# Retention followed by a Fourier mixing block on one core: the eight sums of the second weight's blocks are placed among the third batch's last products

## The chip, the cores and the metric

The kernel runs on one core of a Trainium2 chip. TensorE (PE in the profile) multiplies matrices into PSUM, VectorE (DVE), ScalarE (ACT) and GpSimd (POOL) work element by element, SyncE (SP) issues most transfers. Each engine takes its own instructions strictly in the order of the program, and engines wait for one another by semaphores. The metric is the device time of one execution in microseconds; the median over several runs counts.

## The reference

Four batches of 768 tokens with 8 heads of 64 go through a decaying recurrence, then a Fourier mixing with a normalization, then a two-layer MLP with a residual. Cut to what matters:

```
state = gamma * state + k_t v_t^T ;  y_t = scale * q_t . state      # per head
u  = x + real(fft2(x))                                               # x: y of all heads, 768 x 512
un = (u - mean(u)) / sqrt(var(u) + 1e-6)
out = u + max(un @ w_ch1, 0) @ w_ch2                                 # w_ch1 512 x 2048, w_ch2 2048 x 512
```

## The kernel before

**Batches in a pipeline.** While TensorE runs the MLP of batch b, the recurrence and the mixing of batch b+1 are made between its products. The MLP of batches 0 to 2 is plain: `h_unit` (L1083) makes one block of 128 hidden rows for 384 tokens (four products into one PSUM tile, then a ReLU to `ht16`), and `ch_unit` (L1120) multiplies the hidden rows with the second weight `w216` for 128 tokens: 16 products of 512 columns into the PSUM tile `psc`, and then one VectorE addition at L1131 (`ob` = `psc` times the reciprocal deviation plus `u`) and a store. Three such tiles close a half batch, so batch 2 ends with 48 products and three additions at L1131.

**The last batch is different.** Nothing is left to overlap with it, and its second product is made in a form with seven block products instead of eight (Strassen's scheme in Winograd's form), in three groups g of 256 tokens each. For each group:

- `hp_unit` (L1165), n = 0 to 7: eight products into the PSUM tile `psh` (two hidden blocks, n and n + 8, times 256 tokens), then a ReLU on ScalarE at L1180 into `hg`. For n = 7 the ReLU is cut in two: ScalarE takes the first half (128x256), VectorE the second at L1183. After n = 2, 5 and 7, VectorE forms four differences and sums of the token blocks at L1193 (`s1`, `s2`, `s4`, and one written back into `hg`).
- `p_unit` (L1196), k = 1, 4, 5, 6, 2, 7, 3: seven block products of eight matrix products each (L1217). k = 1, 2 and 3 take a block of `w216` as it is; k = 4, 5, 6 and 7 take one of the sums below. k = 2 goes on in the PSUM tile of k = 1, k = 7 in that of k = 6, and k = 3 in that of k = 5, so each of them must wait until VectorE has read the earlier result (L1222).

**The sums of the weight's blocks.** `wsum_unit` (L1152) makes four differences of 256-column blocks of `w216` (k = 1, 2, 3, 4), each in two parts of four rows of blocks: eight VectorE instructions at L1161, 128x1024 elements of 16 bits each. They are chained: 2 needs 1, 4 needs 2; 3 stands alone. The result tiles come from `inp`, the pool of 11 buffers in which q, k and v arrive; the products k = 4 to 7 of all three groups read them. They depend on nothing of the batch but a free buffer.

**Two halves of the mixing.** The rows of `u` of batch b that the first group needs (blocks kb = 0, 1, 2) are made during batch b - 1. Blocks 3, 4 and 5 are made at the start of batch b's own MLP: `s2_unit` (L991) has four small products into `pq` (L1010), two ScalarE copies (L1012, L1013), two VectorE instructions (L1017, L1020), and two GpSimd additions of x (L1038, L1040); `norm_unit` (L1044) then has the VectorE statistics (L1050, L1051) and the normalization on ScalarE (L1052, `un`); `unT_unit` transposes it by a DMA. For the last batch these blocks 3, 4, 5 stand between the products of its first group, beside the ReLUs and the sums.

**What sets the order.** The units are written out by hand, with a due time each: a stream is a list of units with a start and an end in units of a batch, and `emit` sorts all of them by due time. Then the framework's scheduler arranges the instructions of each engine by its own estimate; it may pull an instruction far forward when nothing holds it. `held` (L148) prevents that for a unit: each of its instructions gets an order dependency on the instruction that stands before it on its engine at the time it is written. (In the program before, `held` is used for the casts of q, k and v.)

**PSUM.** `ps_pm` has three buffers, used in turn by `psc` and `psh`: the three `psc` tiles that close batch 2 are followed, in the same three buffers, by the first three `psh` tiles of batch 3. `ps_g` has five buffers for everything else.

Of the kernel before, what the change touches and what calls it, by code (L numbers as in the profile page):

```python
# [53 lines left out]
LD0, LD1 = (0.223, 0.312), (-0.370, 0.140)  # L54
HT0 = (0.666, 0.693, 0.632, 0.590)
NPE = 2
WS = (0.0, 0.12)
KD = (2, 3)
NT = 0.6
ACT_ROWS = ((2, 5, 6, 7, 8, 9, 10, 14), (0, 3, 6, 7, 9, 10, 11, 12, 14, 15))  # L60
# [3 lines left out]
def kernel(  # L64
# [83 lines left out]
    def held(unit):  # L148
        def run():
            ins = tc.nc.cur_bb.bb.instructions  # L150
            n0 = len(ins)
            unit()
            for n in range(n0, len(ins)):
                m = n - 1
                while m >= 0 and ins[m].engine != ins[n].engine:
                    m -= 1
                if m >= 0:
                    tc.add_manual_dep(ins[n], ins[m].name,
                                      mybir.DependencyInfo(mybir.DependencyClass.NoSync,
                                                           mybir.DependencyReason.DATA),  # L160
                                      reason="casts in turn")
        return run
# [893 lines left out]
    def rstd_unit(b, rt):  # L1056
        def run():
            stats = lb[b]["st"]
            if b == 0 and rt == 0:
                bn_unit(0)()  # L1060
            sl = slice(3 * rt, 3 * rt + 3)
            nc.scalar.activation(stats[:, sl, 2:3], stats[:, sl, 1:2], AF.Sqrt, bias=epsT,
                                 scale=1.0)
            nc.vector.reciprocal(out=stats[:, sl, 3:4], in_=stats[:, sl, 2:3])
        return run

    def unT_unit(b, kb):
        def run():
            un, unT = lb[b].pop(("un", kb)), lb[b]["unT"]
            if b > 1 or b and kb >= 3:  # L1070
                nc.sync.dma_start_transpose(unT[:, :, kb * P:(kb + 1) * P], un)
                return
            pst = ps_g.tile([P, 4, P], f16, tag="g", name="pst", padded_shape=[P, 8, P])
            for cb in range(4):
                nc.tensor.transpose(pst[:, cb, :], un[:, cb * P:(cb + 1) * P], ident16)
            if (kb % 2 == 0) != (b == 0 and kb < 3):
                nc.vector.tensor_copy(unT[:, :, kb * P:(kb + 1) * P], pst)
            else:
                nc.scalar.copy(unT[:, :, kb * P:(kb + 1) * P], pst)
        return run  # L1080
# [61 lines left out]
    def spare(n, name):  # L1142
        return flat(inp.tile([P, 2, NCH, D], f32, tag="in32", name=name))[:, 0:n]
# [5 lines left out]
    def half_of(w, fh, eh, n0, n1):  # L1149
        return w[:, 8 * fh + n0:8 * fh + n1, 256 * eh:256 * eh + 256]  # L1150

    def wsum_unit(k, part):  # L1152


        def run():
            n0, n1 = 4 * part, 4 * part + 4
            t = seven["t", k, part] = spare(4 * 256, "wsum").rearrange("p (n m) -> p n m", n=4)
            a, b = {1: ((0, 1), (0, 0)), 2: ((1, 1), None), 3: ((1, 1), (0, 1)),
                    4: ((1, 0), None)}[k]
            in1 = half_of(w216, *b, n0, n1) if b else seven["t", k // 2, part]  # L1160
            nc.vector.tensor_tensor(out=t, in0=half_of(w216, *a, n0, n1), in1=in1,  # L1161
                                    op=ALU.subtract)
        return run

    def hp_unit(b, g, n):  # L1165

        def run():
            unT = lb[b]["unT"]
            if (g, n) == (0, 0):
                seven["s4"] = spare(8 * P, "s4").rearrange("p (n k) -> p n k", n=8)  # L1170
            psh = ps_pm.tile([P, 2, 256], f32, tag="pm", name="psh")
            for t in range(2):
                fb = n + 8 * t
                for cb in range(4):
                    nc.tensor.matmul(psh[:, t], w116[:, cb, fb * P:(fb + 1) * P],  # L1175
                                     unT[:, cb, g * 256:(g + 1) * 256],
                                     start=(cb == 0), stop=(cb == 3))
            for t0, t1, eng in (((0, 1, "a"), (1, 2, "v")) if n == 7 else ((0, 2, "a"),)):
                if eng == "a":
                    nc.scalar.activation(hg[:, n, t0:t1], psh[:, t0:t1], AF.Relu, bias=0.0,  # L1180
                                         scale=-1.0)
                else:
                    nc.vector.tensor_scalar(out=hg[:, n, t0:t1], in0=psh[:, t0:t1], scalar1=-1.0,  # L1183
                                            scalar2=0.0, op0=ALU.mult, op1=ALU.max)
            if n in (2, 5, 7):
                sl = slice({2: 0, 5: 3, 7: 6}[n], n + 1)
                a11, a12 = hg[:, sl, 0, 0:P], hg[:, sl, 1, 0:P]
                a21, a22 = hg[:, sl, 0, P:256], hg[:, sl, 1, P:256]
                s1, s2, s4 = sg[:, 0, sl], sg[:, 1, sl], seven["s4"][:, sl]
                for out_, x, y, op in ((s1, a21, a22, ALU.add), (s2, s1, a11, ALU.subtract),  # L1190
                                       (s4, a12, s2, ALU.subtract),
                                       (a21, a11, a21, ALU.subtract)):
                    nc.vector.tensor_tensor(out=out_, in0=x, in1=y, op=op)  # L1193
        return run
# [167 lines left out]
    def mix_units(b, kbs, s0, s1, u0, u1):  # L1362
        def turn(j):
            def run():
                s2_unit(b, kbs[j])()
                if j:
                    norm_unit(b, kbs[j - 1])()
            return run
        t = s1 + NT * min((s1 - s0) / 3, u1 - s1)
        return [([turn(j) for j in range(3)], s0, s1), ([norm_unit(b, kbs[2])], t, t),  # L1370
                ([unT_unit(b, kb) for kb in kbs], u0, u1)]
# [21 lines left out]
    streams = []  # L1393
    for b in range(B):
        majors = []
        if b == B - 1:
            for g in range(3):
                majors += [hp_unit(b, g, n) for n in range(8)]
                if g < 2:
                    majors.append(rstd_unit(b, g))  # L1400
                majors += [p_unit(b, g, k) for k in (1, 4, 5, 6, 2, 7, 3)]
            streams.append(([wsum_unit(k, part) for part in range(2) for k in (1, 2, 3, 4)],
                            b + WS[0], b + WS[1]))
        elif b == 0:
            for kb in range(3):
                if kb:
                    majors.append(unT_unit(0, kb))
                majors += [h0_unit(kb, g) for g in range(4)]
        else:
            majors += [h_unit(b, 0, fb) for fb in range(NFB)]  # L1410
        if b < B - 1:
            majors.append(rstd_unit(b, 0))
            majors += [ch_unit(b, 0, rb3, part) for rb3 in range(3) for part in range(4)]
            majors += [h_unit(b, 1, fb) for fb in range(NFB)]
            majors.append(rstd_unit(b, 1))
            majors += [ch_unit(b, 1, rb3, part) for rb3 in range(3) for part in range(4)]
        streams.append((majors, b, b + 1.0))
        streams += mix_units(b, [3, 4, 5], *(b + t for t in (DM0 if b == 0 else DM1)))
        if b + 1 < B:
            steps = attn_steps(b + 1)  # L1420
            if b == 0:
                streams.append(([load_unit(1, i, 6) for i in range(4)], LD0[0], LD0[1]))
                streams.append(([qt_zeros], 0.1, 0.15))
                streams.append(([half_tables], HT0[0], HT0[1]))
                streams.append(([pad_unit], HT0[2], HT0[3]))
                ts = TS0
            else:
                streams.append(([load_unit(b + 1, i) for i in range(4)], b + LD1[0], b + LD1[1]))
                n = [len(u) for u in steps[1:]]
                ts = list(TS1[:2]) + [TS1[2] + TS1[3] * sum(n[:j]) / sum(n) for j in range(6)]  # L1430
            streams.append((steps[0], b + ts[0], b + ts[1]))
            streams += [(u, b + ts[j + 2], b + ts[j + 3]) for j, u in enumerate(steps[1:])]
            end = b + ts[-1]
            da = DA0 if b == 0 else DA1
            sums = [s1_unit(b + 1, e, cb) for cb in range(2) for e in range(2)]
            sums.insert(1, g0_unit(b + 1, (1, 2)))
            streams.append((sums, end + da[0], end + da[1]))
            streams += mix_units(b + 1, [0, 1, 2], *(end + t for t in da[2:]))
# [31 lines left out]
```

## Time and profile before

| what | us |
|---|---|
| median of 3 runs | 242.04 (241.83 to 242.31) |
| the profiled execution | 243.38 |
| its span (first to last instruction) | 240.6 |
| TensorE busy in the span | 226.1 |
| VectorE busy | 189.6 |
| ScalarE busy | 125.2 |
| GpSimd busy | 82.0 |

The profile of one execution is read by several views. The page gives the busy time of each engine, and the chain of work that ended last, followed back from the last instruction. The view of waits says which engine stood idle until which other had finished. The timeline lists each engine's instructions in order of time, merged where equal ones follow each other: the start, the time from the first start to the last end, the engine, line and operation, the tiles, the count, and in brackets the idle time before it and what ended it. The windows give the busy time of each engine in a chosen stretch. In these timelines one instruction's time overlaps the next one's by some 0.05 to 0.1 us, so the step from start to start is a little shorter than the time of a single instruction.

The last batch begins in this span at 194.63 us, when the 48 products that close batch 2 are done; its first group ends at 212.78 us.

### The profile page before, as it was taken

How to read it: one execution, taken by the hardware profiler on the slowest of the kernel's cores; microseconds unless marked ns; L12 is line 12 of the kernel's file. 1: busy time of each engine (PE TensorE's matmuls, PEld its weight loads, DVE VectorE, ACT ScalarE, POOL GpSimd, SP SyncE). 2: the span in 40 equal slices, each digit the busy share in tenths (PEclk: the TensorE clock that was granted, in tenths of full speed). 3: DMA queues.
4: the chain of work that ended last, by engine and by line, in shares of the span. 5: the costliest groups of instructions: out<-in, count | busy, mean ns of one | idle time of the engine just before them, and what ended most of it. 6: DMA issues, size and time to landing. Idle time of an engine off the chain costs nothing.

```text
span 240.6 us, 5573 instructions
## 1 busy us (share of the span) xinstructions
PE 226.1 (94%) x2127; PEld 154.8 (64%) x2127; DVE 189.6 (79%) x472; ACT 125.2 (52%) x272; POOL 82.0 (34%) x148
## 2 busy tenths in 40 slices
PE   0888999999999999999899999999999998899994
PEld 0366779756774656665567446655675477688883
DVE  8699987948898889977886759997886529968473
ACT  5989759675864544931147405822356336251430
POOL 7378802575300197850001817930003204200000
PEclk9999999999999999999999999999999999999999
DMA  7999999999999489979999587675100240140202
GB/s 169 236 269 260 207 207 207 217 245 247 243 232 213 78 193 217 186 142 123 256 277 210 112 177 203 131 120 159 44 3 0 70 131 0 40 115 1 90 0 87
DMA packets 101241, 36.78 MB, mean 153 GB/s; under 512 B 91488, under 2 KB 98528, under 8 KB 101216
## 3 DMA queue, kind: packets, MB, share of 16 engines
q1 hardware_dynamic: 96992, 32.25, 63.5%
q0 software_dynamic: 4224, 4.19, 10.6%
q8 instruction: 16, 0.26, 0.5%
q14 instruction: 9, 0.07, 0.1%
HBM read 27.26 MB, written 6.29 MB: 139 GB/s over the span
## 4 chain that ended last, share of the span: by engine, by line
PE 79%; DVE 7%; DMA 6%; POOL 2%; ACT 2%; issue 1%; SPq 1%; POOLq 0%; DVEq 0%
PE psc L1127 23%; PE psh L1088 21%; PE ps L1217 7%; PE psh L1175 6%; PE psh L1105 3%; PE wkA L665 3%; DMA qTz<-q16z 3%; DMA v<-in_v_dram 3%; PE ps L848 3%; PE wkY L719 2%; PE pq L1010 1%; PE ps L828 1%; PE wkY L715 1%; PE wkK L684 1%; SPq L217 1%
## 5 line engine op out<-in xcount | busy, mean ns | idle before, releaser
L1127 PE MATMUL psc<-w,ht 128*128 128x512 f16 x288 | 67.7, 379 | 0.0
L1088 PE MATMUL psh<-unT,w 128*128 128x384 f16 x320 | 59.5, 326 | 0.0
L1038 POOL TENSOR_TENSOR u<-u,x 128x256 f32<-128x256 f32 x21 | 13.8, 655 | 109.7 <-DVE u L1017 97.4
L1127 PEld LDWEIGHTS <-ht 128*128 128x128 f16 x288 | 27.2, 98 | 26.5
L1088 PEld LDWEIGHTS <-w 128*128 128x128 f16 x320 | 29.9, 98 | 15.9 <-DMA unT<-un 0.4
L1092 ACT ACTIVATE ht<-psh 128x384 f16<-128x384 f32 x46 | 22.3, 489 | 24.1 <-PE psh L1088 23.6
L668 DVE TENSOR_TENSOR atm<-wkA,maskp 128x512 f16<-128x512 f32 x36 | 23.6, 682 | 2.1 <-PE wkA L665 2.1
L1180 ACT ACTIVATE ht<-psh 128x512 f16<-128x512 f32 (+1 forms) x24 | 13.6, 569 | 19.3 <-PE psh L1175 17.1
L1052 ACT ACTIVATE un<-u,stats 128x512 f16<-128x512 f32 x21 | 14.7, 718 | 15.5 <-DVE stats L1051 9.0
L1175 PE MATMUL psh<-unT,w 128*128 128x256 f16 x192 | 22.6, 273 | 0.0
L1131 DVE SCALAR_TENSOR_TENSOR ob<-psc,stats,u 128x512 f32<-128x512 f32 x18 | 13.4, 744 | 9.9 <-PE psc L1127 9.7
L1094 DVE TENSOR_SCALAR ht<-psh 128x384 f16<-128x384 f32 x34 | 18.7, 550 | 2.7 <-PE psh L1088 2.5
L1175 PEld LDWEIGHTS <-w 128*128 128x128 f16 x192 | 18.6, 98 | 2.5 <-DMA unT<-un 0.2
L694 DVE SCALAR_TENSOR_TENSOR s<-s,gk,wkK 128x128 f16<-128x128 f16 x48 | 16.2, 337 | 2.3 <-ACT s L690 1.6
L727 ACT ACTIVATE x<-wkY,gexp 128x384 f16<-128x384 f32 x24 | 12.9, 580 | 9.0 <-PE wkY L719 8.9
L1050 DVE BATCH_NORM_STATS2 bst<-u 128x6 f32<-128x512 f32 x21 | 14.4, 687 | 3.2 <-POOL u L1040 2.8
L1217 PEld LDWEIGHTS <-ht 128*128 128x128 f16 x144 | 13.8, 98 | 4.1 <-ACT ht L1180 1.5
L439 POOL TENSOR_SCALAR kd<-k,gexp 128x384 f16<-128x384 f32 x24 | 13.8, 585 | 3.7 <-DMA k<-in_k_dram 3.6
L1193 DVE TENSOR_TENSOR ht<-ht 128x384 f16<-128x384 f16 (+1 forms) x27 | 9.2, 369 | 6.1 <-ACT ht L1180 5.9
L665 PE MATMUL wkA<-qTz,kT 128*128 128x256 f16 x72 | 13.2, 272 | 0.6 <-DMA qTz<-q16z 0.6
L1040 POOL TENSOR_TENSOR u<-u,x 128x256 f32<-128x256 f32 x21 | 13.4, 640 | 1.0 <-DVE u L1020 1.0
L1217 PE MATMUL ps<-wsum,ht 128*128 128x256 f16 x96 | 12.1, 273 | 0.4 <-DVE ht L1183 0.4
(190 smaller groups left out, 396.3 us busy)
## 6 DMA issues: line engine op xcount, KB each, us to landing
q<-in_q_dram SPq DMA_DIRECT2D x16, 384.0 KB, 5.9
k<-in_k_dram SPq DMA_DIRECT2D x16, 384.0 KB, 5.6
v<-in_v_dram SPq DMA_DIRECT2D x16, 384.0 KB, 5.9
out_dram<-ob SPq DMA_DIRECT2D x21, 256.0 KB, 2.7
w<-in_moe_w_ch_dram POOLq DMA_DIRECT2D x8, 512.0 KB, 10.7
out_dram<-ob SPq DMA_DIRECT2D x5, 128.0 KB, 2.0
unT<-un SPq DMA_TRANSPOSE x15, 2.5
kT<-kd SPq DMA_TRANSPOSE x10, 3.0
```

The lines of the kernel that those rows point to most:

```text
L439: kc = nc.gpsimd.tensor_scalar(out=kd[:, :, h2, :], in0=k32[:, h2], scalar1=gkd[:, h0 + h2:h0 + h2 + 1], scalar2=1.0, op0=ALU.mult, op1=AL ...
L665: mm = nc.tensor.matmul(wk[:, c2], st["kT"][:, c, :], st["qT"][:, :, c, :], start=True, stop=True)
L668: nc.vector.tensor_tensor(out=st["atm"][:, 2 * part:2 * part + 2], in0=wk, in1=maskp[:, PAIR_ORDER[i]].unsqueeze(1).to_broadcast([P, 2, 2, ...
L694: nc.vector.scalar_tensor_tensor(out=s16[:, c], in0=s16[:, c - 1], scalar=gk2[:, hp:hp + 1], in1=wk[:, c - c0], op0=ALU.mult, op1=ALU.add)
L1050: nc.vector.bn_stats(bst, u[:, kb, :])
L1052: nc.scalar.activation(un, u[:, kb, :], AF.Identity, bias=stats[:, kb, 0:1], scale=-1.0)
L1088: nc.tensor.matmul(psh, w116[:, cb, fb * P:(fb + 1) * P], unT[:, cb, rt * 384:(rt + 1) * 384], start=(cb == 0), stop=(cb == 3))
L1092: nc.scalar.activation(ht16[:, fb, :], psh, AF.Relu, bias=0.0, scale=-1.0)
L1094: nc.vector.tensor_scalar(out=ht16[:, fb, :], in0=psh, scalar1=-1.0, scalar2=0.0, op0=ALU.mult, op1=ALU.max)
L1127: nc.tensor.matmul(psc, ht16[:, fb, rb3 * P:(rb3 + 1) * P], w216[:, fb, :], start=(fb == 0), stop=(fb == NFB - 1))
L1175: nc.tensor.matmul(psh[:, t], w116[:, cb, fb * P:(fb + 1) * P], unT[:, cb, g * 256:(g + 1) * 256], start=(cb == 0), stop=(cb == 3))
L1217: nc.tensor.matmul(ps[:, c0:c1], lhsT, rhs[:, c0:c1], start=bool(new and n == 0), stop=(n == 7), skip_group_check=True)
```

## The change

The due times of the eight sums go from 0.0 to 0.12 after the start of the last batch to 0.12 to 0.02 before it, and each sum is held behind the instruction that stands before it on VectorE.

```diff
@@ -54,7 +54,7 @@
 HT0 = (0.666, 0.693, 0.632, 0.590)
 NPE = 2
-WS = (0.0, 0.12)
+WS = (-0.12, -0.02)
 KD = (2, 3)
@@ -1399,7 +1399,7 @@
-            streams.append(([wsum_unit(k, part) for part in range(2) for k in (1, 2, 3, 4)],
+            streams.append(([held(wsum_unit(k, part)) for part in range(2) for k in (1, 2, 3, 4)],
                             b + WS[0], b + WS[1]))
```

## The prediction

> **What bounds the kernel now.** First the page: which engine is full.
>
> ```profile
> PE 226.1 (94%) x2127; PEld 154.8 (64%) x2127; DVE 189.6 (79%) x472; ACT 125.2 (52%) x272; POOL 82.0 (34%) x148
> ```
>
> TensorE sets the end, so moving VectorE work pays only where TensorE waits for it. The view of waits, cut to TensorE from 60 us on, shows where that is; these three are all of 0.3 us or more.
>
> ```profile
> PE ps L1217 <- ACT ht L1180: 1.2, 1, 1.2
> PE wkA L665 <- DMA qTz<-q16z: 0.6, 1, 0.6
> PE ps L1217 <- DVE ht L1183: 0.4, 1, 0.4
> ```
>
> The windows give the stretches around the first and the third.
>
> ```profile
> 184.27:194.63 10.36, 10.36 (x52) 4.70 (x50) 5.50 (x13) 3.04 (x7) 2.62 (x5) 1.00 0.32 87
> 202.31:212.78 10.47, 8.81 (x78) 7.02 (x76) 9.61 (x27) 3.51 (x7) 1.91 (x3) 1.00 0.21 39
> 212.78:237.02 24.24, 24.20 (x230) 21.57 (x227) 15.99 (x43) 8.02 (x15) 0.00 (x0) 1.00 0.14 50
> ```
>
> The columns behind the stretch are its length, then the busy time of PE, PEld, DVE, ACT and POOL. While the third batch's last products run, TensorE is full and VectorE is busy 5.50 of 10.36 us; in the first group of the last batch TensorE loses 1.66 us and VectorE is busy 9.61 of 10.47; behind that TensorE is full again. So the change acts on the 10.47 us. TensorE's timeline of that stretch:
>
> ```profile
> 196.61 1.91 PE L1175 MATMUL psh<-unT,w 128*128 128x256 f16 x16
> ...
> 202.31 0.93 PE L1217 MATMUL ps<-w,ht 128*128 128x256 f16 x7
> 203.07 0.38 PE L1217 MATMUL ps<-wsum,ht 128*128 128x256 f16 x2
> 204.68 0.28 PE L1217 MATMUL ps<-w,ht 128*128 128x256 f16 x1 [1.22 <-ACT ht L1180]
> ...
> 212.78 4.97 PE L1175 MATMUL psh<-unT,w 128*128 128x256 f16 x44
> 217.59 1.04 PE L1217 MATMUL ps<-w,ht 128*128 128x256 f16 x8
> ```
>
> From the last two rows one product of 256 columns takes (217.59 - 212.78)/44 = 0.109 us from start to start. Up to 212.78 there are 56 block products and 20 for the next group, 76 x 0.109 = 8.3 us of work: 2.2 us is idle, which is all that this change could save. The long wait is for the ScalarE half of the ReLU n = 7. Why that is late stands in three engines' timelines, VectorE's first:
>
> ```profile
> 200.12 0.68 DVE L1161 TENSOR_TENSOR wsum<-w 128x1024 f16<-128x1024 f16 x1
> 200.72 0.47 DVE L1017 SCALAR_TENSOR_TENSOR u<-pq,g,qn 128x256 f32<-128x256 f32 x1
> 201.12 0.68 DVE L1161 TENSOR_TENSOR wsum<-w,wsum 128x1024 f16<-128x1024 f16 x1
> 201.72 0.47 DVE L1020 SCALAR_TENSOR_TENSOR u<-pq,g,qn 128x256 f32<-128x256 f32 x1
> 202.11 0.68 DVE L1050 BATCH_NORM_STATS2 bst<-u 128x6 f32<-128x512 f32 x1
> 202.71 0.74 DVE L1161 TENSOR_TENSOR wsum<-w 128x1024 f16<-128x1024 f16 x1
> 203.38 0.17 DVE L1051 BATCH_NORM_AGGREGATE stats<-bst 128x2 f32<-128x6 f32 x1
> 203.47 0.65 DVE L1161 TENSOR_TENSOR wsum<-w,wsum 128x1024 f16<-128x1024 f16 x1
> 204.04 0.35 DVE L1193 TENSOR_TENSOR ht<-ht 128x384 f16<-128x384 f16 x1
> ```
>
> ScalarE's and, below it, GpSimd's:
>
> ```profile
> 203.63 0.72 ACT L1052 ACTIVATE un<-u,stats 128x512 f16<-128x512 f32 x1 [1.40 <-DVE stats L1051]
> 204.26 0.36 ACT L1180 ACTIVATE ht<-psh 128x256 f16<-128x256 f32 x1
> ```
>
> ```profile
> 201.28 1.02 POOL L1038 TENSOR_TENSOR u<-u,x 128x256 f32<-128x256 f32 x1 [1.83 <-DVE u L1017]
> ```
>
> Three sums (200.12, 201.12, 202.71) delay the statistics of block kb = 3; its normalization on ScalarE waits for them until 203.63, and the half ReLU stands behind it in ScalarE's order.
>
> **The change part by part.** Only four of the eight sums are here. The scheduler had already pulled four forward, two at 139 us and two at 158 us (139.04 below is the first); of TensorE's three waits none is near, so taking them away gains nothing. The four in the group cost VectorE 4 x 0.60 = 2.4 us.
>
> *Where the eight go.* The listing of the changed program puts one sum behind the first closing addition (L1131), three behind the reciprocal, four between the second addition and the third. Steps of a sum and an addition, from the early ones:
>
> ```profile
> 139.04 0.77 DVE L1161 TENSOR_TENSOR wsum<-w 128x1024 f16<-128x1024 f16 x1
> 139.73 0.74 DVE L1131 SCALAR_TENSOR_TENSOR ob<-psc,stats,u 128x512 f32<-128x512 f32 x1
> 140.39 0.68 DVE L1161 TENSOR_TENSOR wsum<-w,wsum 128x1024 f16<-128x1024 f16 x1
> ```
>
> And the stretch into which all eight go:
>
> ```profile
> 188.94 0.73 DVE L1131 SCALAR_TENSOR_TENSOR ob<-psc,stats,u 128x512 f32<-128x512 f32 x1
> 190.53 0.18 DVE L1064 RECIPROCAL stats<-stats 128x3 f32<-128x3 f32 x1 [0.86 <-ACT stats L1062]
> 191.37 0.75 DVE L1131 SCALAR_TENSOR_TENSOR ob<-psc,stats,u 128x512 f32<-128x512 f32 x1 [0.66 <-PE psc L1127]
> 194.83 0.75 DVE L1131 SCALAR_TENSOR_TENSOR ob<-psc,stats,u 128x512 f32<-128x512 f32 x1 [2.70 <-PE psc L1127]
> 197.54 0.48 DVE L1017 SCALAR_TENSOR_TENSOR u<-pq,g,qn 128x256 f32<-128x256 f32 x1 [1.96 <-ACT qn L1013]
> ```
>
> An addition steps 0.66 us (139.73 to 140.39), a sum 0.60 (200.12 to 200.72), at most 0.69 (139.04 to 139.73). So sum 1 starts at 189.60; the reciprocal stays at 190.53, since it waits for ScalarE; sums 2 to 4 run from 190.62 to 192.42; the second addition comes 1.05 us late; sums 5 to 8 run from 193.08; the third addition starts at about 195.5 instead of 194.83 and ends at 196.25. Its store is not waited for. Its PSUM buffer is: the third `psh` of the last batch goes into it, at 196.61. That leaves 0.3 us, so I take no wait; with 0.69 for seven sums (7 x 0.09 = 0.6 us more) the product waits some 0.3 us. The idle 1.96 us before 197.54 hides the rest: L1017 stays where it is.
>
> The Trainium skill has a rule against this: "VectorE: DVE Perf Modes", section "Terms", says that the pipe drains behind each operation before the next one can issue. By it a sum would step its whole 0.68 and the third product would wait about 0.3 us (7 x 0.08 less the margin); the trace's steps, 0.60 for 0.68, disagree in this recording.
>
> *What the first group looks like without them.* I walk the listing's order with the steps above; where an instruction waits for another engine I add 0.05 to 0.08 us, as between 203.38 + 0.17 and 203.63. VectorE up to 200.12 is unchanged. Now the statistics of kb = 3 stand there: L1050 at 200.12, L1017 of kb = 4 at 200.72, L1020 at 201.12, the aggregate at 201.51 (before: 203.38). So kb = 3's normalization runs at 201.75. But the listing also changes ScalarE: the two copies for kb = 5 and the ReLU n = 6 now stand behind it (202.81 to 203.41), and then the normalization of kb = 4, **still ahead of the half ReLU n = 7**. That normalization needs two GpSimd additions after L1017 of kb = 4. This row prices them, and those of VectorE what follows:
>
> ```profile
> 186.26 0.64 POOL L1040 TENSOR_TENSOR u<-u,x 128x256 f32<-128x256 f32 x1
> ```
>
> ```profile
> 204.31 0.47 DVE L1017 SCALAR_TENSOR_TENSOR u<-pq,g,qn 128x256 f32<-128x256 f32 x1
> 204.71 1.05 DVE L1193 TENSOR_TENSOR ht<-ht 128x384 f16<-128x384 f16 x2
> 205.69 0.34 DVE L1193 TENSOR_TENSOR s<-ht 128x384 f16<-128x384 f16 x1
> ```
>
> ```profile
> 207.86 0.39 DVE L1183 TENSOR_SCALAR ht<-psh 128x256 f16<-128x256 f32 x1
> ```
>
> GpSimd starts at 201.28 as before and takes 2 x 0.64 (less 0.05 of overlap; the 1.02 of the first one ran beside a sum): done at 202.51. VectorE has nothing else ahead of kb = 4's statistics, so it stands idle from 201.6 to 202.55, with the n = 5 combinations (L1193) queued behind. Statistics 202.55, one L1193 at 203.15, aggregate at 203.42 to 203.59, normalization at 203.67, half ReLU at 204.30 to 204.66, product at **204.72: as late as before (204.68)**. The wait changes its cause and stays. Worse, the two `wsum` products that filled 203.07 to 203.3 now stand behind it, and n = 6 waits for its later ReLU until 203.47: TensorE loses 0.50 + 1.14 us here.
>
> Behind it VectorE goes on with two L1193 at 203.51, the third at 204.49, L1017 and L1020 of kb = 5 at 204.75 and 205.15, then L1183 at 205.55, done at 205.94 (before 208.25). TensorE has made eight products by 205.60 and waits for it until 206.00: 0.40. (Before, products for the next group were placed there.) Ten more products end at 207.2; the next needs an L1193 that stands behind L1222 (205.86) and the statistics of kb = 5 (206.56, when GpSimd is done, to 207.16). At the 0.35 of 204.04 or a little less it ends near 207.45: 0.30 of waiting. After that VectorE's results come within 0.05 us of need. The waits add to 0.50 + 1.14 + 0.40 + 0.30 + 0.05 = 2.4 us against 2.2 before: the group ends **0.2 us later**, and the full TensorE behind it carries that to the end.
>
> *The sum.* 243.38 (span 240.6 plus 2.78 around it) + 0.2 = 243.6 for a profiled execution; the median stands 1.34 below that execution, so 242.04 + 0.2 = 242.3.
>
> Bounds: if all waits behind 204.72 vanished, 0.75 us less, so -0.5; if kb = 4's first GpSimd addition still took 1.02, 0.4 more; with the 0.3 for the PSUM buffer, +0.9 at the top. I take the middle, since the nearest rows are those with no sum alongside. So the forecast's own range is 241.5 to 242.9.
>
> **The rivals.** *The waits go with the sums (faster).* For it: 2.4 us of VectorE time leave a stretch in which VectorE is busy 92%. All 2.2 us saved would be 239.8; half of it, if the ReLU n = 7 came with n = 6 at 203.5, 240.9. Against: ScalarE's listed order, which puts a chain through GpSimd ahead of that ReLU. Anything faster by over 0.2% needs that chain to be shorter than its rows.
>
> *The third closing addition becomes the bound (slower).* Place: the third `psh` at 196.61. It decides as soon as the addition ends after 196.55. With 0.77 for each sum, the longest row, and no overlap, sums 2 to 4 end at 192.93, sums 5 to 8 at 196.67, the addition at 197.42: the product starts 0.85 late, the ReLU n = 2 and all of VectorE's chain with it. 242.04 + 0.85 + 0.2 = 243.1. For it: a margin of only 0.3 us. Against: no sum in the rows steps over 0.69.
>
> *The GpSimd chain is longer than I price it (slower).* With 1.02 for its first addition, 242.04 + 0.6 = 242.7. For it: that is the very row of kb = 4. Against: the sum beside it is gone.
>
> That the change doesn't do what it says holds in part: half the sums never were in the group. It would end at 242.04, within the forecast's case.
>
> **How the numbers follow.** Forecast 0.56; waits go 0.11; third addition 0.17; GpSimd chain 0.16. I call 0.2% (0.48 us) what a measurement can tell from no change. Of the forecast's 0.56, 0.47 lies within it, 0.07 above, 0.02 below. Faster 0.11 + 0.02 = 0.13; same 0.47; slower 0.07 + 0.17 + 0.16 = 0.40. The range runs from 241.5 to 243.2: it takes in both slower rivals and leaves out the faster one and the far ends.
>
> **What would show it.** Right: in the first group, L1052 of kb = 4 directly ahead of the half ReLU on ScalarE, with VectorE's L1050 released by POOL L1040 near 202.5, and TensorE's product near 204.7 released by L1180. Right: no wait at the third `psh` near 196.6, and a new wait of about 0.4 us for L1183 near 206. Wrong: a wait of L1175 for DVE L1131 (second rival), or the half ReLU ending before 204 (first rival).

## The result and the profile after

| | before | changed |
|---|---|---|
| median of 14 runs each, us | 242.27 | 241.50 (241.26 to 242.17) |
| ratio of the two, 95% interval | | 0.997 (0.996 to 0.998) |
| profiled execution, us | 243.38 | 241.30 |
| its span, us | 240.6 | 239.4 |

The change makes the kernel some 0.7 us faster in this comparison; 0.2 us slower was forecast. The median lies at the lower end of the range, and the sign is wrong. The view of waits of the changed kernel, cut to TensorE from 60 us on (engine, line, what it waited for: us in total, times, longest):

```profile
PE ps L1217 <- ACT ht L1180: 1.3, 2, 1.0
PE ps L848 <- DVE ee L785: 0.2, 1, 0.2
```

Of the three waits shown of before, the one for the half ReLU is still there, the one for VectorE's half (L1183) is gone, and the one for a transfer at L665 is not there in this execution either. The whole span is 1.2 us shorter, so the first question is in which stretch. TensorE does the same products in both kernels from the first product of the last batch up to the first product of its third group; the windows give that stretch and the rest up to the end, first of before, then of the changed kernel:

```profile
194.63:223.70 29.07, 27.41 (x253) 23.74 (x252) 23.22 (x59) 12.16 (x26) 4.28 (x6) 1.00 0.16 45
223.70:240.60 16.90, 13.29 (x130) 11.81 (x127) 8.47 (x24) 4.56 (x8) 0.00 (x0) 0.99 0.17 59
```

```profile
193.68:222.54 28.86, 27.43 (x253) 23.83 (x252) 21.42 (x57) 12.25 (x26) 3.80 (x6) 1.00 0.16 47
222.54:239.40 16.86, 13.28 (x130) 11.81 (x127) 8.47 (x24) 4.56 (x8) 0.00 (x0) 0.98 0.17 59
```

The stretch is 28.86 us in place of 29.07: **0.21 us shorter, where my walk had it 0.2 us longer**. The rest is equal within 0.04. The other 0.95 us lies ahead of the last batch (194.63 against 193.68), where the order of TensorE's instructions is the same in both. Whether that belongs to the change was the first thing to test.

TensorE's timeline of the first group in the changed kernel:

```profile
193.68 1.91 PE L1175 MATMUL psh<-unT,w 128*128 128x256 f16 x16
...
201.36 0.82 PE L1217 MATMUL ps<-w,ht 128*128 128x256 f16 x6
202.49 0.28 PE L1217 MATMUL ps<-w,ht 128*128 128x256 f16 x1 [0.31 <-ACT ht L1180]
203.76 0.28 PE L1217 MATMUL ps<-w,ht 128*128 128x256 f16 x1 [0.99 <-ACT ht L1180]
203.88 2.88 PE L1217 MATMUL ps<-wsum,ht 128*128 128x256 f16 x22
206.60 0.27 PE L1175 MATMUL psh<-unT,w 128*128 128x256 f16 x1
```

The products of n = 6 and n = 7 wait as forecast. The 22 products behind 203.88 show no wait for L1183. At 0.109 us each they would be done by 206.28, and the next starts at 206.60, so about 0.3 us of waiting is hidden inside. The timeline of TensorE's weight loads (PEld, one ahead of each product) shows it behind the eighteenth of them: the load waits for VectorE's L1193, as forecast.

```profile
206.15 0.33 PEld L1217 LDWEIGHTS <-ht 128*128 128x128 f16 x4 [0.41 <-DVE ht L1193]
```

ScalarE's timeline has the normalization of kb = 4 directly ahead of the half ReLU:

```profile
202.72 0.72 ACT L1052 ACTIVATE un<-u,stats 128x512 f16<-128x512 f32 x1 [0.28 <-issue]
203.35 0.36 ACT L1180 ACTIVATE ht<-psh 128x256 f16<-128x256 f32 x1
```

VectorE's timeline shows why L1183 was in time:

```profile
201.59 0.70 DVE L1050 BATCH_NORM_STATS2 bst<-u 128x6 f32<-128x512 f32 x1 [0.86 <-POOL u L1040]
202.20 0.34 DVE L1193 TENSOR_TENSOR ht<-ht 128x384 f16<-128x384 f16 x1
202.46 0.18 DVE L1051 BATCH_NORM_AGGREGATE stats<-bst 128x2 f32<-128x6 f32 x1
202.58 0.63 DVE L1193 TENSOR_TENSOR ht<-ht 128x384 f16<-128x384 f16 x2
203.12 0.35 DVE L1193 TENSOR_TENSOR s<-ht 128x384 f16<-128x384 f16 x1
...
204.18 0.42 DVE L1183 TENSOR_SCALAR ht<-psh 128x256 f16<-128x256 f32 x1
```

The pair of L1193 at 202.58 steps 203.12 - 202.58 = 0.54 us. I had priced it 0.98, from the pair at 204.71 of before. GpSimd's timelines, first of before and then of the changed kernel, show the difference between the two pairs:

```profile
204.86 0.68 POOL L1038 TENSOR_TENSOR u<-u,x 128x256 f32<-128x256 f32 x1 [1.96 <-DVE u L1017]
```

```profile
200.33 0.64 POOL L1038 TENSOR_TENSOR u<-u,x 128x256 f32<-128x256 f32 x1 [1.82 <-DVE u L1017]
200.92 0.64 POOL L1040 TENSOR_TENSOR u<-u,x 128x256 f32<-128x256 f32 x1
203.95 0.64 POOL L1038 TENSOR_TENSOR u<-u,x 128x256 f32<-128x256 f32 x1 [2.39 <-DVE u L1017]
```

In before, a GpSimd addition began 0.15 us after the pair. In the changed kernel GpSimd stands idle from 201.56 to 203.95, the whole time of the pair. That the addition beside it made the difference is still only read from two rows here; an experiment below tests it.

### The profile page after: what moved, and what is told of

Its sections match the earlier page's. It is cut to its first block, busy times and chain, and to the rows that moved or that the text cites. A ratio compares the mean times of both kernels' runs of the same rounds, so it can differ in the third digit from the quotient of the medians.

```text
span 239.4 us, 5574 instructions
## 1 busy us (share of the span) xinstructions
PE 226.8 (95%) x2127; PEld 155.5 (65%) x2127; DVE 189.6 (79%) x472; ACT 125.2 (52%) x272; POOL 81.6 (34%) x148
## 4 chain that ended last, share of the span: by engine, by line
PE 85%; DVE 7%; ACT 2%; DMA 2%; issue 1%; POOL 1%; SPq 0%; DVEq 0%; ACTq 0%
PE psc L1127 25%; PE psh L1088 21%; PE psh L1175 7%; PE ps L1217 7%; PE psh L1105 3%; PE wkA L665 3%; PE ps L848 3%; PE ps L828 2%; PE wkY L719 2%; DMA k<-in_k_dram 2%; PE pq L1010 1%; PE wkY L715 1%; PE wkK L684 1%; PE wps L172 1%; PE pq L922 1%
## 5 line engine op out<-in xcount | busy, mean ns | idle before, releaser
L1038 POOL TENSOR_TENSOR u<-u,x 128x256 f32<-128x256 f32 x21 | 13.3, 635 | 109.9 <-DVE u L1017 97.5
L1180 ACT ACTIVATE ht<-psh 128x512 f16<-128x512 f32 (+1 forms) x24 | 13.7, 570 | 20.2 <-PE psh L1175 20.2
L1050 DVE BATCH_NORM_STATS2 bst<-u 128x6 f32<-128x512 f32 x21 | 14.4, 688 | 3.9 <-POOL u L1040 3.7
L1193 DVE TENSOR_TENSOR ht<-ht 128x384 f16<-128x384 f16 (+1 forms) x27 | 8.8, 353 | 8.3 <-ACT ht L1180 8.0
L1040 POOL TENSOR_TENSOR u<-u,x 128x256 f32<-128x256 f32 x21 | 13.4, 640 | 0.0
L665 PE MATMUL wkA<-qTz,kT 128*128 128x256 f16 x72 | 13.2, 272 | 0.0
```

The lines of the kernel that those rows point to most:

```text
L665: mm = nc.tensor.matmul(wk[:, c2], st["kT"][:, c, :], st["qT"][:, :, c, :], start=True, stop=True)
L1050: nc.vector.bn_stats(bst, u[:, kb, :])
```

## The experiments

"Stretch" is the time from the first product of the last batch to the first of its third group, as above. The kernels with a ratio were run beside the kernel before on the same chip, in three sets (one line apart in the table).

| kernel | median us (runs) | ratio to before, 95% | stretch, us |
|---|---|---|---|
| before, again | 242.45 (12) | 0.9999 (0.9979 to 1.0019) | 29.08 |
| changed, again | 241.87 (12) | 0.9981 (0.9965 to 0.9997) | 28.85 |
| unheld | 241.96 (12) | 0.9992 (0.9973 to 1.0011) | 28.85 |
| held, at the old place | 242.70 (12) | 1.0010 (0.9996 to 1.0024) | 29.61 |
| | | | |
| changed, third | 241.57 (12) | 0.9967 (0.9950 to 0.9984) | 28.85 |
| normalizations later | 241.85 (12) | 0.9976 (0.9959 to 0.9994) | 28.73 |
| mixing later | 241.59 (12) | 0.9980 (0.9955 to 1.0004) | 28.60 |
| GpSimd additions | 243.42 (1) | | 30.52 |
| | | | |
| changed, fourth | 241.78 (12) | 0.9976 (0.9962 to 0.9991) | 28.86 |
| mixing at the seam | 240.29 (6) | 0.9917 (0.9894 to 0.9940) | 27.58 |
| mixing between | 241.53 (12) | 0.9965 (0.9949 to 0.9981) | 28.53 |

**Both kernels again.** No edit.

> The kernel before, unchanged, for spans and a second profile. Theory A (the gain lies in the first group of the last batch alone, some 0.25 us in the two first profiles; the other 0.95 us between their spans came before 117 us and is chance): the spans scatter by some 0.7 us around 240, the last batch takes 45.9 us from its first product to the end of the span, and the 0.65 us wait of L665 for a transposed q at 116 us is in some executions only. Theory B (the change also saves about 0.5 us elsewhere, between the first product and the start of the last batch): the last batch begins at 194.4 to 194.6 us here and at 193.7 in the changed kernel again, by the same wait.

> The changed kernel, unchanged. Theory A: the last batch takes 45.7 us from its first product to the end, 0.2 to 0.3 less than before; its median beside that of the kernel before is 0.2 to 0.5 us lower. Theory B: 0.7 us lower again, and the last batch begins 0.5 us earlier than before in this profile too.

The stretch repeats to 0.01 us: 29.07 and 29.08 of before, 28.86 and 28.85 of the changed kernel. The start of the last batch doesn't repeat: 194.63 and 194.02 us before, 193.68 and 194.00 after (194.16 and 194.43 in the later profiles of the changed kernel). Nor does the wait for the transfer at L665: 0.6 and 0.2 us in the two profiles of before, and in the four of the changed kernel none, 0.3, 0.2 and 0.6. **So the 0.95 us ahead of the last batch in the first pair of profiles is scatter between executions, and the change is worth 0.22 us of its stretch.** The third comparison, with its ratio of 0.9967, lies below the 0.998 to 0.9995 that I had expected if the first group's gain were all; the section behind the experiments says what is left over.

**The sums early, but not held; and held, at the old place.** These take the two halves of the change apart.

```diff
-WS = (0.0, 0.12)
+WS = (-0.12, -0.02)
```

> The due times of the change without the hold: the scheduler then spreads all eight sums between 138 and 166 us; the other engines' orders are those of the changed kernel. If what counts is only that no sum stands in the first group (and the order that the scheduler then gives it), this is as fast as the changed kernel, within 0.2 us. If it counts that they stand among the last products of the third batch, it is slower than that by 0.3 us or more.

```diff
-            streams.append(([wsum_unit(k, part) for part in range(2) for k in (1, 2, 3, 4)],
+            streams.append(([held(wsum_unit(k, part)) for part in range(2) for k in (1, 2, 3, 4)],
```

> The hold without the new due times: all eight sums at the start of the last batch, three of them right behind the third closing addition and five beside the first group. VectorE has 0.6 us per sum more to do there than in the kernel before. Theory A says that this stretch is bound by VectorE's chain to the half ReLU n = 7: four more sums of which two stand ahead of it: 0.5 to 1.5 us slower than the kernel before. Rival (the wait is set by GpSimd and ScalarE, sums are free): within 0.2 us of it.

Without `held` the scheduler spreads the eight sums over 138 to 166 us, and the stretch is the changed kernel's, 28.85: where in the third batch they stand is indifferent, since nothing waits for them there. Its time (0.9992) is not told apart from either kernel's. Held at the old place all eight stand in the first group and the stretch is 29.61. So eight sums in the group cost 0.54 us more than the four of before, the low end of the 0.5 to 1.5 that I had expected, and none 0.22 less. The time of the held kernel (1.0010) isn't told apart from that of before. TensorE's waits in the held kernel:

```profile
PE ps L1217 <- ACT ht L1180: 1.3, 1, 1.3
PE ps L1217 <- DVE ht L1183: 0.9, 1, 0.9
```

The wait for L1180 is 1.2 to 1.3 us with none, four or eight sums in the group. What the sums change is the wait for L1183: 0.9 with eight, 0.4 with four, none with none. Part of it is a matter of order: with them in the group the scheduler also puts L1183 on VectorE behind the statistics of kb = 4 and 5 (two L1050 at 206.35 in before, at 206.46 here), and without them ahead of those of kb = 5. Two rows of this kernel, VectorE's and GpSimd's, show a sum and a GpSimd addition slowing each other, against 0.68 and 0.64 each alone:

```profile
203.10 1.12 DVE L1161 TENSOR_TENSOR wsum<-w,wsum 128x1024 f16<-128x1024 f16 x1
```

```profile
202.60 1.08 POOL L1040 TENSOR_TENSOR u<-u,x 128x256 f32<-128x256 f32 x1
```

**GpSimd additions beside L1193.** This measures the mis-priced term by itself. In the last batch's second group, where GpSimd has nothing to do, three additions stand ahead of each set of four L1193 (the line is L1198 here, and L1222 is L1227):

```diff
+                if g == 1:
+                    old = lb[2]["u"]
+                    for _ in range(3):
+                        nc.gpsimd.tensor_tensor(out=old[:, 0, 0:256], in0=old[:, 1, 0:256],
+                                                in1=hg[:, n, 1, :], op=ALU.add)
                 for out_, x, y, op in ((s1, a21, a22, ALU.add), (s2, s1, a11, ALU.subtract),
...
```

> The changed kernel with three extra GpSimd additions of two tiles (128x256, f32 and f16, into the dead u tile of the third batch) issued beside each set of the four combinations L1193 of the last batch's second group, nine in all; the output doesn't depend on them. It measures by itself the price that my forecast took for two L1193. Theory: a pair of 128x384 additions takes 0.54 to 0.63 us alone and 0.98 to 1.05 us beside GpSimd, as in the row I priced it from, because GpSimd's addition runs at the same time; so some of the L1193 of that group measure 0.45 us or more for 128x384, in place of 0.34. Rival: the long pair had another cause (its place behind another operation, its wait), and the L1193 of that group keep 0.34 to 0.36 us each beside the GpSimd additions.

The groups of that line, cut to the second group (213 to 222 us) and then to the third, which has no such additions (226 to 240 us); behind the bar are the busy time, the mean ns of one, and the idle time before:

```profile
L1198 DVE TENSOR_TENSOR ht<-ht 128x384 f16<-128x384 f16 x6 | 3.6, 630 | 2.6 <-ACT ht L1180 2.6
L1198 DVE TENSOR_TENSOR s<-ht 128x384 f16<-128x384 f16 x2 | 1.7, 826 | 0.0
```

```profile
L1198 DVE TENSOR_TENSOR ht<-ht 128x384 f16<-128x384 f16 x6 | 2.0, 356 | 4.2 <-ACT ht L1180 4.2
L1198 DVE TENSOR_TENSOR s<-ht 128x384 f16<-128x384 f16 x2 | 0.7, 351 | 0.0
```

The same instruction takes 356 ns alone and 630 to 826 ns on average beside GpSimd. GpSimd's three take 0.78 us each, against 0.64 for its additions of f32 tiles with nothing beside them (these have one 16-bit operand, and their time alone isn't measured):

```profile
213.61 2.34 POOL L1193 TENSOR_TENSOR u<-u,ht 128x256 f32<-128x256 f32 x3 [7.82 <-ACT ht L1180]
```

And the second group, in which the changed kernel has no wait, now has two, so the stretch is 30.52 us, 1.67 longer:

```profile
PE ps L1222 <- DVE ht L1183: 0.6, 1, 0.6
PE ps L1222 <- DVE u L1227: 0.4, 1, 0.4
```

The rival (another cause of the long pair) falls, and a late L1193 does make TensorE wait for L1183 (0.6 us). The row of before from which I took 0.98 held a collision that the change removes.

**What the remaining 1.3 us are worth: the mixing of kb 4 and 5 moved behind the first group.** The wait for the half ReLU was put down to the chain of kb = 4 ahead of it on ScalarE. Four placements test that. First the normalizations alone:

```diff
+        late = b == B - 1 and kbs[0] == 3
...
-                if j:
+                if j and not (late and j == 2):
...
+        if late:
+            return [([turn(j) for j in range(3)], s0, s1),
+                    ([held(norm_unit(b, kb)) for kb in kbs[1:]], b + 0.30, b + 0.42),
+                    ([unT_unit(b, 3)], u0, b + 0.268),
+                    ([unT_unit(b, kb) for kb in kbs[1:]], b + 0.42, b + 0.50)]
```

> The changed kernel with the statistics and normalizations of blocks kb 4 and 5 of the last batch moved behind the first group, so that the half ReLU n = 7 stands directly behind the ReLU n = 6 on ScalarE. Theory: what is left of the group's idle time in the changed kernel is the wait for that half ReLU behind kb = 4's normalization (0.31 + 0.99 us). Then the half ReLU ends about 0.9 us earlier, TensorE's list of waits from 60 us on shows for L1180 at most 0.5 us in place of 1.3, and the time is 0.6 to 1.0 us below the changed kernel's, some 241.0 us. Rival: VectorE's own order (the combinations L1193 and the half ReLU L1183 behind L1017 and L1020 of kb = 5) is nearly as late: the wait moves to L1183 or L1193, 0.5 to 1.0 us, and the time stays within 0.3 us of the changed kernel's. If VectorE's statistics in the second group come too late for its products, the time rises.

Then the products, copies and combinations of kb 4 and 5 as well:

```diff
+            return [([turn(0)], s0, b + 0.048), ([norm_unit(b, 3)], b + 0.09, b + 0.09),
+                    ([held(s2_unit(b, 4)), held(s2_unit(b, 5))], b + 0.34, b + 0.42),
+                    ([held(norm_unit(b, kb)) for kb in kbs[1:]], b + 0.42, b + 0.48),
...
```

> As the kernel before it in this set, but the combining of kb 4 and 5 (L1017, L1020 and the two copies on ScalarE) is moved behind the first group too, so that nothing but ReLUs and combinations stands in that group on ScalarE and VectorE behind kb = 3. Theory that those operations are the whole cause of the group's idle time: no wait of 0.3 us or more in the group, the time 1.0 to 1.4 us below the changed kernel's, about 240.6 us. Rival: they were hidden once the normalizations are away, so the time equals that kernel's within 0.2 us. Second rival: the second group, in which VectorE is busy two thirds of the time, can't take them in: new waits there, time no better than the changed kernel's.

In both, the half ReLU comes directly behind the ReLU n = 6 and the wait for L1180 shrinks from 1.3 us to 0.3 and 0.2: the chain of kb = 4 was its cause. But the stretch gains only 0.12 and 0.25 us over the changed kernel, where I had expected 0.6 to 1.4 of the time. In the first a new wait for L1222 takes part of it, so its rival was right that the time stays within 0.3 us of the changed kernel's, though it named other instructions:

```profile
PE ps L1217 <- DVE u L1222: 0.3, 1, 0.3
PE ps L1217 <- ACT ht L1180: 0.3, 1, 0.3
```

TensorE's timeline of the second of these kernels shows where the rest goes:

```profile
202.88 2.81 PE L1217 MATMUL ps<-wsum,ht 128*128 128x256 f16 x24
205.64 1.03 PE L1217 MATMUL ps<-w,ht 128*128 128x256 f16 x8
206.81 1.03 PE L1217 MATMUL ps<-wsum,ht 128*128 128x256 f16 x8
...
216.94 2.78 PE L1217 MATMUL ps<-wsum,ht 128*128 128x256 f16 x24
219.97 1.03 PE L1217 MATMUL ps<-w,ht 128*128 128x256 f16 x8 [0.25 <-DVE u L1222]
220.84 0.27 PE L1217 MATMUL ps<-w,s 128*128 128x256 f16 x1
221.14 1.03 PE L1217 MATMUL ps<-wsum,ht 128*128 128x256 f16 x8
```

By 0.109 us a product, 0.14 and 0.30 us are idle ahead of 205.64 and 206.81, where TensorE waits for VectorE to read a result (L1222) and no product of the next group is placed in between any more; 0.41 ahead of 219.97 and 0.19 ahead of 221.14 are new. In the second group L1222 stands on VectorE behind the reciprocal L1064 at 218.49, which needs the statistics of kb = 5, now made late. My second rival for that kernel held: the second group couldn't take the work where it was put. So the next two kernels change nothing but the due times, to 0.26, 0.30, 0.34, 0.38 ("at the seam") and 0.30, 0.36, 0.38, 0.44 ("between"):

> As the kernel that moved the combining and normalizations of kb 4 and 5 behind the first group, but with earlier due times, so that they lie at the seam of the first and the second group, and the reciprocal of the second group (L1064), which waits for the last of their statistics, stands before that group's first combinations. Theory: that kernel lost in the second group what it had won in the first (0.41 and 0.19 us of gaps in TensorE's timeline there, the first by the view of waits on L1222, which stood behind the reciprocal at 218.49), so with the reciprocal early no wait for L1222 is left in the second group; from the last batch's first product to the end 45.0 us, against 45.4 and, in the changed kernel, 45.7; time some 0.5 to 0.7 us below the changed kernel's, about 241.0. Rival: the statistics delay the second group's combinations instead, a wait of 0.3 us or more for L1193 or L1180 there, and no gain on the earlier placement.

> The same with due times between those two: the normalizations before the last two ReLUs of the second group, the reciprocal directly behind L1183. Theory: the reciprocal ends about 1.3 us earlier than in the first placement and L1222 is in time; the second group's wait for L1222 (0.25 us) is gone, the time 0.3 to 0.6 us below the changed kernel's. Rival: as for the kernel before, the two statistics of 0.68 us delay the combinations of n = 3 to 5 behind them, and the gain is at most 0.2 us.

> The changed kernel unaltered, beside the two others: 45.7 us from the last batch's first product to the end of the span, ratio to the kernel before 0.997 to 0.999.

At the seam the stretch is 27.58 us, 1.28 below the changed kernel's, and the median falls to **240.29 us: 0.9917 of before (0.9894 to 0.9940), faster than both kernels**. I had expected 0.5 to 0.7 us. TensorE's timeline shows the further half: the small products of kb 4 and 5 (L1010, `pq`) now fill the two gaps of the first group at 205.28 and 206.39, where the kernel before it in the series stood idle, and no gap is left in the second.

```profile
202.64 2.81 PE L1217 MATMUL ps<-wsum,ht 128*128 128x256 f16 x24
205.28 0.39 PE L1010 MATMUL pq<-gk,g16r 128*128 128x129 f16 x4
205.51 1.03 PE L1217 MATMUL ps<-w,ht 128*128 128x256 f16 x8
206.39 0.39 PE L1010 MATMUL pq<-gk,g16r 128*128 128x129 f16 x4
206.62 1.03 PE L1217 MATMUL ps<-wsum,ht 128*128 128x256 f16 x8
```

In the placement between, only 0.33 us of the 1.28 are gained (28.53), the low end of what I had expected: the wait for L1222 is gone, but there the products of `pq` come after the gaps, and the ReLU n = 6 of the second group is late (a wait of 0.25 us for L1180).

## Why the prediction was wrong

**Right: the early sums and the third addition.** The sums step 0.60 to 0.61 us (189.70 to 190.31 below), 0.72 where one needs the one directly before it (192.17 to 192.89). VectorE's timeline of the changed kernel:

```profile
189.70 0.69 DVE L1161 TENSOR_TENSOR wsum<-w,wsum 128x1024 f16<-128x1024 f16 x1
190.31 0.69 DVE L1161 TENSOR_TENSOR wsum<-w 128x1024 f16<-128x1024 f16 x1
...
192.17 0.69 DVE L1161 TENSOR_TENSOR wsum<-w 128x1024 f16<-128x1024 f16 x1
192.89 0.69 DVE L1161 TENSOR_TENSOR wsum<-w,wsum 128x1024 f16<-128x1024 f16 x1
...
194.71 0.75 DVE L1131 SCALAR_TENSOR_TENSOR ob<-psc,stats,u 128x512 f32<-128x512 f32 x1
```

The third addition ends at 195.46, ahead of the third `psh` at 195.66, without a wait: a margin of 0.2 us where I had 0.3. The second rival falls, and so does the rule that I took from one line of the Trainium skill ("VectorE: DVE Perf Modes", section "Terms") and set against the trace: here too a sum that needs nothing from the one before it steps 0.60 for its 0.69.

**Right: the wait changes its cause and stays.** Counted from the first product of the last batch, I had the product of n = 6 at 203.47 - 194.63 = 8.84 us and that of n = 7 at 204.72 - 194.63 = 10.09; measured are 8.81 and 10.08 (before: 10.05). L1050 of kb = 4 was released by GpSimd's L1040, and the half ReLU stood behind kb = 4's normalization. Moving that normalization took 1.0 of the 1.3 us away, which shows the cause. The first rival (all waits go with the sums) falls: the half ReLU's wait stayed, and only the one for L1183 went. The third (a longer GpSimd addition) falls too: 0.64 measured at 200.33, not 1.02.

**Wrong: the new wait for L1183, 0.40 us.** It didn't come. The step that failed is "two L1193 at 203.51, the third at 204.49": 0.98 us for the pair, from the row at 204.71 that I quoted. It measured 0.54, so L1183 ended at 204.60, 10.92 us after the batch's start in place of 11.31. The eighth of the 22 products behind 203.88 is the one that reads L1183's half; it was due at 203.88 + 7 x 0.109 = 204.64, so the half came 0.04 us ahead of it. By this arithmetic, with the pair at 0.98 it would have ended at 205.04, and the 0.40 us of the forecast would have been there; no run puts the collision back into this group. I had cleaned the GpSimd row of the sum beside it (1.02 to 0.64) and didn't ask the same of the VectorE row: GpSimd's timeline of before has the addition at 204.86 in the middle of the pair.

**The account.** My waits were 0.50 + 1.14 + 0.40 + 0.30 + 0.05 = 2.4 us. By the changed kernel's timeline they are 0.48 (up to 202.49), 1.16 (up to 203.76), none, and 0.32 (up to 206.60): 1.96 us, against 2.2 of before. The sign of the group's part hung on one mis-sized term: with 0.54 for the pair the group gains 0.2 us, as measured, in place of losing 0.2. (242.04 + 0.2 is 242.24, where I had written 242.3; that changes nothing.)

**The size.** The four comparisons gave ratios from 0.9967 to 0.9981, some 0.6 us on average. The stretch explains 0.22. The span medians differ by 0.2 to 0.3 us within a set (240.0 to 240.1 of before; 239.55 to 239.9 of the changed kernel over all sets), which is near it. The rest lies outside the span: the device time less the span has medians of 2.03 to 2.16 us with the kernel before and 1.88 to 1.92 with the changed one. It was above 2.4 us in 34 of 99 executions of before and in none of 50 of the changed kernel. It doesn't hang on the place of the sums alone: with all eight held at the old place it was above 2.4 us in none of 12 executions, with the early sums not held in 2 of 12. What happens there is not in the trace, and it stays open. The prediction carried it over unchanged ("2.78 around it") without a reason.

## What to carry to other kernels

Before a duration of VectorE or GpSimd is taken from a row, look at what the other one does in that time, on both sides of the change: a row that holds a collision prices the collision. What moving work off a busy engine gains depends on what the waiting engine waits for last. Here the chain of kb = 4 set that, and moving the mixing of kb 4 and 5 to the seam of two groups, where its own products fill gaps of TensorE, was worth six times the change (1.28 us against 0.22). And a difference ahead of the place of the change, in one pair of profiles, needs a second pair before it is explained.

## What the hardware showed

A VectorE addition of two 16-bit tiles from SBUF and a GpSimd addition from SBUF slow each other: 0.36 us became 0.63 to 0.83 on average for VectorE's 128x384 beside three GpSimd additions, and 0.64 became 1.08 for GpSimd's 128x256 beside a sum. L1222, which has one operand in PSUM, doesn't show it: in the changed kernel it took 0.75 us beside a GpSimd addition (first row and second) and 0.75 without one (third row, where GpSimd has no more work):

```profile
204.50 0.75 DVE L1222 SCALAR_TENSOR_TENSOR u<-ps,stats,u 128x512 f32<-128x512 f32 x1
```

```profile
204.54 0.64 POOL L1040 TENSOR_TENSOR u<-u,x 128x256 f32<-128x256 f32 x1
```

```profile
217.77 0.75 DVE L1222 SCALAR_TENSOR_TENSOR u<-ps,stats,u 128x512 f32<-128x512 f32 x1
```

The Trainium skill ("SBUF — State Buffer", section "Who interferes with whom") says that a VectorE instruction contends with a GpSimd instruction that reads SBUF where both its inputs lie in SBUF, and, outside its 2-port modes, not where at most one does. Both halves agree with these rows.
